# Pair weights loaded product by product, signs made on ScalarE, and a pause for weight sums: three edits to a fused attention and two feed-forward blocks

## The chip, the cores and the metric

The program runs on one core of a Trainium2 chip. Five engines work side by side, each through its own list of instructions in order: PE (TensorE, matrix products, with its weight loads shown as PEld), DVE (VectorE), ACT (ScalarE), POOL (GpSimd) and SP (SyncE, which here only issues DMA transfers). They meet at semaphores. The metric is the device time of one execution in microseconds (us).

## What is computed

The chunked attention of the reference gives 3072 tokens of width 512, which pass a gated block with 1536 hidden columns and then a second block with 2048:

```python
def _moe_ref(x, w_gate, w_val, w_out, rms_g):
    xn = x / np.sqrt(np.mean(x * x, axis=-1, keepdims=True) + 1e-06) * rms_g
    g = xn @ w_gate
    silu = g * (1.0 / (1.0 + np.exp(-g)))
    return silu * (xn @ w_val) @ w_out

def _moe2_ref(x, w_in, w_out):            # beta = 1
    h = x @ w_in
    g = np.where(h >= 1, h, np.where(h <= -1, 0.0, (h + 1) ** 2 / 4.0))
    return g @ w_out
```

## The kernel before, in words

**Numbers.** Every matrix product is split: each operand is a high part and a low part (the remainder), and three 128x128 by 128x512 matmuls stand for one product block. The weights arrive as float64, two 32-bit words for each number. A conversion takes an ACT pass over the high word (`conv_c` and `c`, lines 132 and 289, a scaled copy into a tile `tu`), three DVE operations that put exponent, sign and the low word's bits together (`join`, lines 142, 145, 148), an ACT copy that makes the high part (`hi`, line 292) and a DVE subtraction that makes the low part (`lo`, line 295).

**Token tiles.** The tokens form six tiles of 512. In the *single stage* (0 to about 518 us) four of them go through the first block one at a time: 12 feature steps `f`, each of three slots, with the attention of later tokens woven in between. The last two tiles, and all six tiles of the second block, go in pairs by a scheme with seven products in place of eight (`seven`): for each step the weights of seven products are needed, some of them sums and differences of weight blocks. The *pair input stage* of the first block (518 to 655 us) has 12 such units of 7 products of 6 matmuls; the *pair output stage* of it follows (to 718.7 us); then three pairs go through the second block (to 1194.4 us).

**Weight sums.** The seven weights of each unit (`w1p_d`, `w2p_d`, `w1o_d`, `w2o_d`) are made ahead of time by small steps: `at(n, fn)` puts a function on step `n`, and `conv_step(pace)` runs `pace` steps on average. In the last three single tiles each slot runs 2.8 steps, in the pair input stage each product runs `PACE2` steps; `conv_step(len(bg))` behind that stage runs all that is left. A group of 28 steps handles four float64 tiles of the second block: load (`load_w2`, POOL's queue), conversion, and two `pair_sums` of six steps (steps 10 to 15), whose results go to DRAM through POOL's queue. While a `pair_sums` is open, its name stands in `live`.

**Loading.** `load_wp(n)` brings the seven weights of unit `n` (1792 KB) through SP's queue into one half of a two-part buffer, which lies where the single tiles' weights of the features 9 to 11 were. It is issued at the end of unit `n - 2`. `load_wo` brings the output weights. The engines' orders are the order in which the code is written (`manual_schedule`), so an instruction that waits holds all that stand behind it on its engine; SP's and POOL's queues do the same with transfers.

In a unit, bank B starts as a copy of bank A (line 908, on ACT), the product in C is copied out (line 909, on ACT), and products are added on top:

```python
        product(n, A, 0, 0, True)
        product(n, C, 3, 2, True)
        p5 = tmp2("p5")
        nc.scalar.activation(B, A, AF.Copy)
        nc.scalar.activation(p5, C, AF.Copy)
        ...
        tt(out=C, in0=p5, in1=B, op=ALU.add)
```

Of the kernel before, what the change touches and what calls it, by code (L numbers as in the profile page):

```python
# [8 lines left out]
F32 = mybir.dt.float32  # L9
# [7 lines left out]
P = 128  # L17
# [16 lines left out]
D = 64  # L34
FILL = 352
PACE = 2.8
PACE2 = 0.9


@with_exitstack  # L40
def tile_stream_attention_moe_moe2(
# [85 lines left out]
    def conv_c():  # L127


        dst, key, w64 = raw.pop(0)  # L130
        tu = tmp.tile([P, 512], U32, tag="tu", name="tu")
        nc.scalar.activation(tu.bitcast(F32), words(w64)[1].bitcast(F32), AF.Copy, scale=2.0 ** -112)
        absd.append((dst, key, w64, tu))

    def words(w64):
        w = w64.rearrange("p (n two) -> p n two", two=2)
        return w[:, :, 0], w[:, :, 1]

    def join(tu, w64):

        lo64, hi64 = words(w64)
        nc.vector.tensor_scalar(
            out=tu, in0=tu, scalar1=3, scalar2=0x7FFFFFF8, op0=ALU.logical_shift_left, op1=ALU.bitwise_and
        )
        nc.vector.scalar_tensor_tensor(
            out=tu, in0=hi64, scalar=0x80000000, in1=tu, op0=ALU.bitwise_and, op1=ALU.bitwise_or
        )
        nc.vector.scalar_tensor_tensor(
            out=tu, in0=lo64, scalar=29, in1=tu, op0=ALU.logical_shift_right, op1=ALU.bitwise_or
        )  # L150
# [27 lines left out]


    G2 = F2 // 2  # L180
    w2p_d = [dram.tile([P, 2, 7, 256], F32, name=f"w2p_d{g}") for g in range(G2)]
    w2o_d = [dram.tile([P, 7, 2, 2, 256], F32, name=f"w2o_d{g}") for g in range(G2 // 2)]

    w1p_d = [dram.tile([P, 2, 7, 256], F32, name=f"w1p_d{f}") for f in range(F1)]
    w1o_d = [dram.tile([P, 7, 2, 2, 256], F32, name=f"w1o_d{k}") for k in range(F1 // 4)]


# [19 lines left out]
            nc.gpsimd.dma_start(dst(n, k), src.rearrange("p (k c) -> p k c", k=2))  # L209

    def in_dst(dp):
        return lambda n, k: dp[:, n, 3 + 2 * k:5 + 2 * k]

    def out_dst(do, u):
        return lambda n, k: do[:, (1, 4)[k]:(3, 6)[k], u, n]
# [42 lines left out]
    def w1_steps(i, f):  # L258
        g, v = (unit(3 * f + k).bitcast(F32) for k in range(2))
        dp = w1p_d[f]  # L260
        raws = [(dp[:, :, 0:2].rearrange("p h k c -> p h (k c)"), g), (dp[:, :, 2], v[:, :, 256:512])]
        sum_steps(i, (g, v), raws, rows_order, in_dst(dp))

    def w1o_steps(i, k):
# [15 lines left out]
    def w2_steps(g):  # L280

        dp, do, u = w2p_d[g], w2o_d[g // 2], g % 2
        f32_ = {}

        part = lambda j, n: w2raw[j][:, 512 * n:512 * n + 512]

        def c(j):
            f32_[j] = tmp.tile([P, 512], U32, tag="tu", name="tu")
            nc.scalar.activation(f32_[j].bitcast(F32), words(w2raw[j])[1].bitcast(F32), AF.Copy, scale=2.0 ** -112)

        def hi(j, n0, n1):
            nc.scalar.activation(part(j, 0)[:, n0:n1].bitcast(F32R), f32_[j].bitcast(F32)[:, n0:n1], AF.Copy)

        def lo(j, n0, n1, dsts):
            tt_(
                out=part(j, 1)[:, n0:n1].bitcast(F32),
                in0=f32_[j].bitcast(F32)[:, n0:n1],
                in1=part(j, 0)[:, n0:n1].bitcast(F32),
                op=ALU.subtract,
            )  # L300
            src = w2raw[j].bitcast(F32).rearrange("p (h c) -> p h c", h=2)
            for dst, c0, c1 in dsts:
                nc.gpsimd.dma_start(dst, src[:, :, c0:c1])

        dsts = [
            [(dp[:, :, 0:2].rearrange("p h k c -> p h (k c)"), 0, 512)],
            [(dp[:, :, 2], 256, 512)],
            [(do[:, 0, u], 0, 256)],
            [(do[:, 3, u], 0, 256), (do[:, 6, u], 256, 512)],
        ]  # L310
        for k in range(4):
            j, n = 4 * g + k, W2 + 28 * g + 7 * k
            n0, n1 = ((0, 512), (256, 512), (0, 256), (0, 512))[k]
            at(n, lambda j=j: c(j))
            at(n + 2, lambda j=j: join(f32_[j], w2raw[j]))
            at(n + 3, lambda j=j, n0=n0, n1=n1: hi(j, n0, n1))
            at(n + 5, lambda j=j, n0=n0, n1=n1, k=k: lo(j, n0, n1, dsts[k]))
            at(n + 10, lambda j=j: load_w2(j + 3))
        def pair_sums(a, b, n, order, dst):
            S, h = [], lambda: (f32_[a], f32_[b])  # L320

            def first():
                if m2["single"]:
                    S.extend([sp.tile([P, TT], F32, tag="s", name="s12"), sums_.tile([P, TT], F32, tag="s34", name="s34")])
                else:
                    S.extend(m2["late"][:, i] for i in range(2))
                S[:] = [x.rearrange("p (k c) -> p k c", k=2) for x in S]
                live.append(a)
                sums(S, *order(h()), True)

            at(n + 10, first)
            at(n + 11, lambda: sums(S, *order(h()), False))
            at(n + 12, lambda: hi_s(S, 0, f32_[a]))
            at(n + 13, lambda: hi_s(S, 1, f32_[b]))
            at(n + 14, lambda: lo_s(S, 0, f32_[a], dst))
            at(n + 15, lambda: (lo_s(S, 1, f32_[b], dst), live.remove(a)))

        pair_sums(4 * g, 4 * g + 1, W2 + 28 * g, rows_order, in_dst(dp))
        pair_sums(4 * g + 2, 4 * g + 3, W2 + 28 * g + 14, cols_order, out_dst(do, u))
# [442 lines left out]


    xb = wall[:, 0:14]
    wp = wall[:, 14:21].rearrange("p a b c -> p (a b c)").rearrange(
        "p (n h k c) -> p n h k c", n=2, h=2, k=7
    )
    wo = {}
    NP2 = NTT // 2

# [2 lines left out]
            nc.sync.dma_start(m2["y"][:, o], src[o])  # L793


    def load_wp(n):
        if n < F1 + NP2 * G2:
            src = w1p_d[n] if n < F1 else w2p_d[(n - F1) % G2]
            nc.sync.dma_start(wp[:, n % 2].bitcast(F32), src)

    def load_wo(i):

# [44 lines left out]
    for t in range(NS):  # L847
# [3 lines left out]
        for f in range(F1):  # L851
            if 0 < t < NS - 1 and f == 9:
                load_x(t + 1)
            if t == NS - 1 and f == F1 - 1:
                load_wp(0)
            proj_in(ps_g[0], w1[("g", f)])
            s = sp.tile([P, TT], F32, tag="s", name="s")
            nc.scalar.activation(s, ps_g[0], AF.Silu)  # L858
# [15 lines left out]
                out1(*pend)  # L874
            pend = (t, f)
            slot(t, 3 * f + 2)
    load_wp(1)

    b1, b2 = ps_g

    def product(n, bank, a, x, start):

        for kk in range(2):
            sl = slice(kk * P, kk * P + P)
            wh, wl = (wp[:, n % 2, i, a, sl] for i in range(2))
            xh, xl = (xb[:, 2 * x + kk, i] for i in range(2))
            st = start and kk == 0
            nc.tensor.matmul(bank, wh, xh, start=st, stop=False, skip_group_check=True)  # L888
            nc.tensor.matmul(bank, wh, xl, start=False, stop=False, skip_group_check=True)  # L889
            nc.tensor.matmul(bank, wl, xh, start=False, stop=kk == 1, skip_group_check=True)  # L890
        if n < F1:
            conv_step(PACE2)

    def tmp2(name):
# [5 lines left out]
    def seven(n, early):  # L900

        A, B, C, D, E = banks
        banks[:] = D, A, E, C, B
        tt = nc.vector.tensor_tensor
        product(n, A, 0, 0, True)
        product(n, C, 3, 2, True)
        p5 = tmp2("p5")
        nc.scalar.activation(B, A, AF.Copy)  # L908
        nc.scalar.activation(p5, C, AF.Copy)
        while defer:  # L910
            defer.pop(0)()
        product(n, B, 4, 1, False)
        product(n, A, 1, 4, False)
        tt(out=C, in0=p5, in1=B, op=ALU.add)
        done11 = early(A)
        product(n, B, 5, 3, False)
        tt(out=p5, in0=p5, in1=B, op=ALU.add)
        product(n, C, 6, 5, False)
        product(n, B, 2, 6, False)
        return done11, C, B, p5  # L920

    def t3(k):
# [3 lines left out]
    def proj1(f):  # L926
        k, u = divmod(f, 2)

        def silu(z):
            s = tmp2("s")  # L930
            nc.scalar.activation(s, z, AF.Silu)
            return s

        gate0, z12, z21, val1 = seven(f, silu)
        gate1 = silu(z12)
        tt_(out=m2["h"][:, k, u, 0], in0=gate0, in1=z21, op=ALU.mult)
        tt_(out=m2["h"][:, k, u, 1], in0=val1, in1=gate1, op=ALU.mult)
        if u:
            t3(k)
        load_wp(f + 2)  # L940

    def proj2(n):
        k = n % G2
# [157 lines left out]
    out1(*pend)  # L1101
    while live:
        conv_step(1)
    m2["single"] = False
    single_only.close()
    pair1 = moe1_only.enter_context(ExitStack())
    m2["pool"] = pair1.enter_context(tc.tile_pool(name="p1", bufs=1, reuse_waits="tile"))
# [144 lines left out]
```

## Time and profile before

| what | value |
|---|---|
| median of 3 runs | 1203.23 us (1202.67 to 1204.07) |
| the profiled execution's own time | 1202.52 us |
| its span in the trace | 1200.8 us |
| PE busy | 1144.0 us (95%) |
| DVE busy | 865.3 us (72%) |
| ACT busy | 620.2 us (52%) |
| POOL busy | 156.5 us (13%) |
| DMA moved | 281.76 MB, mean 235 GB/s |

A busy share is a mean over stages that have different limits, and a PE at half its clock is busy as well. So the table says which engine has the most to do, and not where time is lost; for that the span is cut into the stages named above.

### The profile page before, as it was taken

What the parts mean: (1) busy time and instruction counts of PE and PEld (TensorE: products, weight loads), DVE (VectorE), ACT (ScalarE), POOL (GpSimd) and SP (SyncE); (2) the same over time, 40 slices, a digit from 0 to 9 for tenths busy, and PEclk for the clock granted to TensorE, in tenths of its full rate; (3) what the DMA queues carried; (4) which work ended last, traced back from release to release, by engine and by line L of the source; (5) the groups of instructions that cost most, each with busy time, mean ns of one, the idle gap of its engine ahead of it and who ended that gap; (6) DMA issues with size and microseconds to landing.
All of it is one profiled execution on the core that took longest, in us unless ns stands there. A gap on an engine that the chain in (4) does not pass through costs nothing. (4 is left out here: it accounts for less than half of the span.)

```text
span 1200.8 us, 20562 instructions
## 1 busy us (share of the span) xinstructions
PE 1144.0 (95%) x7909; PEld 915.6 (76%) x7909; DVE 865.3 (72%) x1494; ACT 620.2 (52%) x1096; POOL 156.5 (13%) x239
## 2 busy tenths in 40 slices
PE   7889999999999999988998989999999999999998
PEld 4677878887777778766776868778887787887886
DVE  5888876676657767865655776787857888578855
ACT  4766756565666665433332644446534455444543
POOL 2200012231323233321221000000000000000000
PEclk8899999999999999998998999999999999999999
DMA  8565468898868777698896666656756476653465
GB/s 300 178 212 203 148 245 284 274 324 288 299 219 281 251 253 248 242 340 292 329 328 228 217 217 227 259 218 188 218 178 265 182 224 199 192 208 137 140 193 158
DMA packets 93968, 281.76 MB, mean 235 GB/s; under 512 B 11440, under 2 KB 34480, under 8 KB 87472
## 3 DMA queue, kind: packets, MB, share of 16 engines
q1 hardware_dynamic: 66992, 207.05, 51.2%
q0 software_dynamic: 19200, 65.03, 15.2%
q10 hardware_dynamic: 7680, 8.39, 2.0%
q8 instruction: 62, 1.02, 0.4%
q14 instruction: 34, 0.28, 0.1%
HBM read 201.26 MB, written 79.17 MB: 234 GB/s over the span
## 5 line engine op out<-in xcount | busy, mean ns | idle before, releaser
L1047 PE MATMUL ps_y<-r,wo 128*128 128x512 f32 x720 | 169.3, 391 | 2.6 <-DVE r L997 1.6
L997 DVE TENSOR_TENSOR r<-h,r 128x512 fp32r<-128x512 f32 x180 | 120.8, 688 | 54.4 <-ACT r L995 54.4
L1047 PEld LDWEIGHTS ps_y<-r,wo 128*128 128x128 f32 x720 | 134.3, 188 | 33.3 <-DVE r L997 3.3
L584 PE MATMUL ps_g<-xh,wall 128*128 128x512 f32 x384 | 157.1, 409 | 2.2 <-ACT s L858 2.1
L585 PE MATMUL ps_g<-xl,wall 128*128 128x512 f32 x384 | 151.1, 394 | 0.0
L586 PE MATMUL ps_g<-xh,wall 128*128 128x512 f32 x384 | 150.9, 393 | 0.0
L995 ACT ACTIVATE r<-h 128x512 fp32r<-128x512 f32 x180 | 108.3, 624 | 62.8 <-DVE h L986 15.0
L948 ACT ACTIVATE t<-t,half 128x512 f32<-128x512 f32 x96 | 66.9, 720 | 128.6 <-DVE t L947 128.6
L1047 PE MATMUL ps_g<-r,wo 128*128 128x512 f32 x540 | 127.4, 392 | 1.2 <-DVE r L997 1.1
L1047 PEld LDWEIGHTS ps_g<-r,wo 128*128 128x128 f32 x540 | 100.6, 188 | 24.9 <-DVE r L997 3.8
L888 PE MATMUL ps_g<-wall 128*128 128x512 f32 x198 | 80.4, 406 | 8.5 <-ACT ps_g L908 6.8
L584 PEld LDWEIGHTS ps_g<-xh,wall 128*128 128x128 f32 x384 | 73.0, 190 | 19.2 <-ACT s L858 2.9
L586 PEld LDWEIGHTS ps_g<-xh,wall 128*128 128x128 f32 x384 | 72.9, 190 | 16.5 <-DVE wall L117 0.4
L888 PE MATMUL ps_b<-wall 128*128 128x512 f32 x202 | 79.8, 395 | 5.2 <-DMA wall<-w1p_d 4.9
L585 PEld LDWEIGHTS ps_g<-xl,wall 128*128 128x128 f32 x384 | 73.0, 190 | 13.4
L584 PE MATMUL ps_y<-hh,wall 128*128 128x512 f32 x192 | 78.2, 407 | 2.8 <-ACT hh L116 2.8
L889 PE MATMUL ps_b<-wall 128*128 128x512 f32 x202 | 79.2, 392 | 0.0
L890 PE MATMUL ps_b<-wall 128*128 128x512 f32 x202 | 79.1, 392 | 0.0
L889 PE MATMUL ps_g<-wall 128*128 128x512 f32 x198 | 78.4, 396 | 0.0
L890 PE MATMUL ps_g<-wall 128*128 128x512 f32 x198 | 78.3, 395 | 0.0
L585 PE MATMUL ps_y<-hl,wall 128*128 128x512 f32 x192 | 75.7, 394 | 0.2 <-DVE hl L117 0.2
L586 PE MATMUL ps_y<-hh,wall 128*128 128x512 f32 x192 | 75.6, 394 | 0.0
(179 smaller groups left out, 2145.5 us busy)
## 6 DMA issues: line engine op xcount, KB each, us to landing
wo<-w2o_d SPq DMA_DIRECT2D x88, 512.0 KB, 3.7
wall<-w2p_d SPq DMA_DIRECT2D x24, 1792.0 KB, 7.3
wall<-w1p_d SPq DMA_DIRECT2D x12, 1792.0 KB, 10.2
w<-in_w_dram SPq DMA_DIRECT2D x36, 512.0 KB, 3.7
w<-in_w_dram POOLq DMA_DIRECT2D x32, 512.0 KB, 5.0
k_in<-in_k_dram SPq DMA_DIRECT2D x48, 256.0 KB, 4.7
wo<-w1o_d SPq DMA_DIRECT2D x21, 512.0 KB, 3.8
v_in<-in_v_dram SPq DMA_DIRECT2D x40, 260.0 KB, 4.4
```

Source lines behind the costliest of these rows:

```text
L584: nc.tensor.matmul(ps, wh, xh, start=start, stop=False)
L585: nc.tensor.matmul(ps, wh, xl, start=False, stop=False)
L586: nc.tensor.matmul(ps, wl, xh, start=False, stop=stop)
L888: nc.tensor.matmul(bank, wh, xh, start=st, stop=False, skip_group_check=True)
L889: nc.tensor.matmul(bank, wh, xl, start=False, stop=False, skip_group_check=True)
L890: nc.tensor.matmul(bank, wl, xh, start=False, stop=kk == 1, skip_group_check=True)
L948: nc.scalar.activation(s, s, AF.Square, scale=0.5, bias=half)
L995: nc.scalar.activation(r[:, 0], src, AF.Copy)
L997: tt_(out=r[:, 1], in0=src, in1=r[:, 0].bitcast(F32), op=ALU.subtract)
L1047: nc.tensor.matmul(bank[p][m], a, b, start=s0, stop=s1, skip_group_check=True)
```

## The change

Three things change together.

1. The pair weights lie in DRAM product by product (`[P, 7, 2, 256]` in place of `[P, 2, 7, 256]`), and are loaded one product (256 KB) at a time into a ring of 14. The load of product `i + 14` stands right behind product `i`. Eight loads are issued at the last feature step of the last single tile and six behind it. The writes of the sums into DRAM follow the new layout in runs of 1 KB where they had 2 KB, and the two writes of raw weights into such a unit become three.
2. The ACT pass over the high word uses `Prelu`, whose slope for negative input is 2^32. This moves the exponent of a negative number so that the shift by 3 puts a bit into the sign's place; `join` loses its sign operation, and has two DVE operations in place of three.
3. In the last seven slots of the last single tile no step is run unless a `pair_sums` is open. `PACE2` goes from 0.9 to 0.95, and each `load_w2` stands three steps later in its group.

```diff
-PACE2 = 0.9
+PACE2 = 0.95
...
-        nc.scalar.activation(tu.bitcast(F32), words(w64)[1].bitcast(F32), AF.Copy, scale=2.0 ** -112)
+        nc.scalar.activation(tu.bitcast(F32), words(w64)[1].bitcast(F32), AF.Prelu, scale=2.0 ** -112, alpha=2.0 ** 32)
...
-        nc.vector.tensor_scalar(
-            out=tu, in0=tu, scalar1=3, scalar2=0x7FFFFFF8, op0=ALU.logical_shift_left, op1=ALU.bitwise_and
-        )
-        nc.vector.scalar_tensor_tensor(
-            out=tu, in0=hi64, scalar=0x80000000, in1=tu, op0=ALU.bitwise_and, op1=ALU.bitwise_or
-        )
+        nc.vector.tensor_scalar(out=tu, in0=tu, scalar1=3, scalar2=None, op0=ALU.logical_shift_left)
...
-    w1p_d = [dram.tile([P, 2, 7, 256], F32, name=f"w1p_d{f}") for f in range(F1)]
+    w1p_d = [dram.tile([P, 7, 2, 256], F32, name=f"w1p_d{f}") for f in range(F1)]
...
-            at(n + 10, lambda j=j: load_w2(j + 3))
+            at(n + 13, lambda j=j: load_w2(j + 3))
...
             m2["pace"] -= 1
+            if m2["hold"] and not live:
+                continue
...
+            m2["hold"] = t == NS - 1 and s >= 29
             conv_step(PACE)
...
-    def load_wp(n):
+    def load_wp(i):
+        n, j = divmod(i, 7)
         if n < F1 + NP2 * G2:
             src = w1p_d[n] if n < F1 else w2p_d[(n - F1) % G2]
-            nc.sync.dma_start(wp[:, n % 2].bitcast(F32), src)
+            nc.sync.dma_start(wp[:, i % 14].bitcast(F32), src[:, A_OF[j]])
...
             if t == NS - 1 and f == F1 - 1:
-                load_wp(0)
+                for i in range(8):
+                    load_wp(i)
...
-        if n < F1:
+        load_wp(i + 14)
+        if i < 7 * F1:
             conv_step(PACE2)
```

Where the steps go follows from the paces. Before, 304 steps stand ahead of the pair input stage, the other 72 lie in it, and none is left behind it. After, 282 stand ahead of it, 80 lie in it, and the last 17 run in one piece behind it.

On DVE, at the end of the pair input stage, before (`h` are the hidden values, `y` the next tile's input, `r` the ring from which the output products read):

```order
L936 TENSOR_TENSOR h<-t_6062,ps_g_108 128x512
L937 TENSOR_TENSOR h<-t_6061,t_6057 128x512
L924 TENSOR_TENSOR h<-h 128x512
L834 TENSOR_TENSOR y<-y 128x1024
L997 TENSOR_TENSOR r_6067<-h,r_6067 128x512
L999 TENSOR_TENSOR h<-h 128x512
```

The same place on DVE after the change:

```order
L926 TENSOR_TENSOR h<-h 128x512
L290 TENSOR_TENSOR w_6762<-tu,w_6762 128x256
L142 TENSOR_SCALAR tu<-tu 128x512
L143 SCALAR_TENSOR_TENSOR tu<-w_6833,tu 128x512
L192 TENSOR_TENSOR s_5971<-tu 128x256
L193 TENSOR_TENSOR s_5971<-tu 128x256
L195 TENSOR_TENSOR s_5971<-s_5971,tu 128x256
L196 TENSOR_TENSOR s_5971<-tu,s_5971 128x256
L290 TENSOR_TENSOR w_6833<-tu,w_6833 128x512
L202 TENSOR_TENSOR s_5971<-s_5971,tu 128x512 x2
L833 TENSOR_TENSOR y<-y 128x1024
L997 TENSOR_TENSOR r_5982<-h,r_5982 128x512
```

Ten operations of the left-over steps now stand between the last hidden values and the first ring entry of the output stage.

On SP, at the passage from the single tiles to the pair, before (`ys` is the last single tile's result, `wo` the output weights):

```order
L799 DMA wall_102<-w1p_d0_132 128x3584
L799 DMA wall_102<-w1p_d1_133 128x3584
L618 DMA y_d3_113<-ys_6034 128x2048
L815 DMA wo_6075<-w1o_d0_144 128x1024
L815 DMA wo_6077<-w1o_d1_145 128x1024
L815 DMA wo_6079<-w1o_d2_146 128x1024
L815 DMA wo_6081<-w1o_d0_144 128x1024
L799 DMA wall_102<-w1p_d2_134 128x3584
```

The same place on SP after the change:

```order
L798 DMA wall_102<-w1p_d0_132 128x512 x7
L798 DMA wall_102<-w1p_d1_133 128x512 x7
L613 DMA y_d3_113<-ys_5957 128x2048
L814 DMA wo_5990<-w1o_d0_144 128x1024
L814 DMA wo_5992<-w1o_d1_145 128x1024
L814 DMA wo_5994<-w1o_d2_146 128x1024
L814 DMA wo_5996<-w1o_d0_144 128x1024
L798 DMA wall_102<-w1p_d2_134 128x512 x7
```

The places are the same; each load of a unit has become seven, each of which stands behind one product of two units earlier.

On ACT, in the last two feature steps of the single stage, before (`s` is the gate, `hh` the high part of the hidden values, `w` a float64 tile of the second block):

```order
L292 ACTIVATE w_5766<-tu 128x512
L858 ACTIVATE s<-ps_g_108 128x512
L204 ACTIVATE tu<-s_5884 128x512
L204 ACTIVATE tu<-s_5885 128x512
L116 ACTIVATE hh<-s 128x512
L824 ACTIVATE wall<-y 128x2x512
L289 ACTIVATE tu<-w_5838 128x512
L292 ACTIVATE w_5838<-tu 128x512
L858 ACTIVATE s<-ps_g_108 128x512
```

The same place on ACT after the change:

```order
L823 ACTIVATE wall<-y 128x2x512
L858 ACTIVATE s<-ps_g_108 128x512
L116 ACTIVATE hh<-s 128x512
L823 ACTIVATE wall<-y 128x2x512
L858 ACTIVATE s<-ps_g_108 128x512
L116 ACTIVATE hh<-s 128x512
```

The conversions and sums between the gates and the hidden values are gone from there.

## Rows read from the trace of the kernel before

**Rows 1.** Busy time by stage: stretch, length, each engine, granted clock, DMA share, GB/s.

```profile
498.00:518.00 20.00, 15.09 (x51) 11.29 (x50) 17.83 (x30) 8.05 (x14) 6.16 (x9) 0.84 0.89 323
518.00:655.00 137.00, 121.61 (x506) 97.20 (x505) 76.63 (x133) 47.78 (x86) 30.68 (x47) 0.95 0.84 302
655.00:718.70 63.70, 60.35 (x254) 46.63 (x253) 49.25 (x70) 33.30 (x53) 0.00 (x0) 1.00 0.69 218
718.70:1194.40 475.70, 473.00 (x2106) 385.70 (x2104) 355.11 (x552) 226.18 (x364) 0.00 (x0) 1.00 0.60 201
```

**Rows 2.** Timeline of PE in the single stage's last steps: start, length, work, idle before.

```profile
500.23 0.50 PE L584 MATMUL ps_g<-xh,wall 128*128 128x512 f32 x1 [1.90 <-ACT s L858]
```

**Rows 3.** Timeline of ACT just ahead of it.

```profile
499.06 0.63 ACT L292 ACTIVATE w<-tu 128x512 fp32r<-128x512 f32 x1 [2.73 <-issue]
499.60 0.58 ACT L858 ACTIVATE s<-ps_g 128x512 f32<-128x512 f32 x1
```

**Rows 4.** Busy time of PE alone behind that wait: busy, clock, DMA share, GB/s.

```profile
501.00:504.50 3.50, 3.50 (x10) 0.54 0.99 415
```

**Rows 5.** Waits of PE in the pair input stage: total us, times, longest.

```profile
PE ps_g L888 <- ACT ps_g L908: 6.8, 2, 5.0
PE ps_b L888 <- DMA wall<-w1p_d: 4.9, 1, 4.9
```

**Rows 6.** Timeline of SP's queue in that stage.

```profile
531.66 1.34 SPq L815 DMA_DIRECT2D wo<-w1o_d  x3
533.11 7.33 SPq L799 DMA_DIRECT2D wall<-w1p_d  x2
```

**Rows 7.** Timeline of ACT, POOL and DVE in that stage.

```profile
524.35 0.60 ACT L909 ACTIVATE t<-ps_b 128x512 f32<-128x512 f32 x1 [1.52 <-DMA y_d<-ys]
...
618.95 0.56 POOL L276 DMA_DIRECT2D w<-in_w_dram  x1 [10.77 <-DMA w2p_d<-w]
...
628.97 0.66 ACT L289 ACTIVATE tu<-w 128x512 f32<-128x512 f32 x1 [4.16 <-DMA w2p_d<-tu]
...
634.72 0.43 DVE L197 TENSOR_TENSOR s<-tu 128x256 f32<-128x256 f32 x1
634.77 0.63 ACT L292 ACTIVATE w<-tu 128x512 fp32r<-128x512 f32 x1 [4.13 <-issue]
```

**Rows 8.** Groups by line and shape, whole span: busy us, mean ns, idle before.

```profile
L145 DVE SCALAR_TENSOR_TENSOR tu<-w,tu 128x512 uint32<-128x512 uint32 x68 | 48.6, 717 | 1.6
L142 DVE TENSOR_SCALAR tu<-tu 128x512 uint32<-128x512 uint32 x68 | 28.9, 429 | 14.6 <-ACT tu L289 9.5 <-ACT tu L132 5.0
L289 ACT ACTIVATE tu<-w 128x512 f32<-128x512 f32 x32 | 21.2, 662 | 15.7 <-DMA w2p_d<-tu 7.4 <-DMA w2o_d<-tu 5.1 <-DMA w<-in_w_dram 3.2
L948 ACT ACTIVATE t<-t,half 128x512 f32<-128x512 f32 x96 | 66.9, 720 | 128.6 <-DVE t L947 128.6
```

**Rows 9.** Transfers of the pair input stage: all, then one kind, us to landing.

```profile
DMA packets 7211, 41.35 MB, mean 302 GB/s; under 512 B 1073, under 2 KB 1073, under 8 KB 5397
...
w2p_d<-tu POOLq DMA_DIRECT2D x6, 256.0 KB, 7.9
```

**Rows 10.** Transfers issued in the first 20 us, us to landing.

```profile
k_in<-in_k_dram SPq DMA_DIRECT2D x8, 256.0 KB, 4.9
```

**Rows 11.** Busy time by stretch in the opening, columns as in rows 1.

```profile
10.00:15.00 5.00, 2.53 (x107) 1.83 (x110) 2.05 (x4) 1.78 (x3) 0.00 (x0) 0.82 1.06 396
```

**Rows 12.** Timeline of DVE at the start of the pair output stage.

```profile
657.05 1.22 DVE L834 TENSOR_TENSOR y<-y 128x1024 f32<-128x1024 f32 x1
658.19 0.68 DVE L997 TENSOR_TENSOR r<-h,r 128x512 fp32r<-128x512 f32 x1
```

**Rows 13.** Waits of PE from 40 to 489 us, first and last of eight rows.

```profile
PE ps_a L557 <- ACT xn L573: 3.3, 1, 3.3
...
PE ps_a L461 <- ACT x_nat L573: 0.6, 1, 0.6
```

**Rows 14.** Timeline of ACT ahead of one of these waits.

```profile
416.30 0.42 ACT L292 ACTIVATE w<-tu 128x256 fp32r<-128x256 f32 x1 [2.59 <-DVE tu L148]
```

More of the change, by code (lines that the diff above doesn't have):

```diff
@@ L139, in join @@
     def join(tu, w64):
-        lo64, hi64 = words(w64)
-        nc.vector.tensor_scalar(
-            out=tu, in0=tu, scalar1=3, scalar2=0x7FFFFFF8, op0=ALU.logical_shift_left, op1=ALU.bitwise_and
-        )
-        nc.vector.scalar_tensor_tensor(
-            out=tu, in0=hi64, scalar=0x80000000, in1=tu, op0=ALU.bitwise_and, op1=ALU.bitwise_or
-        )
+        lo64 = words(w64)[0]
+        nc.vector.tensor_scalar(out=tu, in0=tu, scalar1=3, scalar2=None, op0=ALU.logical_shift_left)
         nc.vector.scalar_tensor_tensor(
@@ L180, in tile_stream_attention_moe_moe2 @@
     G2 = F2 // 2
-    w2p_d = [dram.tile([P, 2, 7, 256], F32, name=f"w2p_d{g}") for g in range(G2)]
+    w2p_d = [dram.tile([P, 7, 2, 256], F32, name=f"w2p_d{g}") for g in range(G2)]
     w2o_d = [dram.tile([P, 7, 2, 2, 256], F32, name=f"w2o_d{g}") for g in range(G2 // 2)]
-    w1p_d = [dram.tile([P, 2, 7, 256], F32, name=f"w1p_d{f}") for f in range(F1)]
+    w1p_d = [dram.tile([P, 7, 2, 256], F32, name=f"w1p_d{f}") for f in range(F1)]
     w1o_d = [dram.tile([P, 7, 2, 2, 256], F32, name=f"w1o_d{k}") for k in range(F1 // 4)]
@@ L211, in in_dst @@
     def in_dst(dp):
-        return lambda n, k: dp[:, n, 3 + 2 * k:5 + 2 * k]
+        return lambda n, k: dp[:, 3 + 2 * k:5 + 2 * k, n]
     def out_dst(do, u):
@@ L260, in w1_steps @@
         dp = w1p_d[f]
-        raws = [(dp[:, :, 0:2].rearrange("p h k c -> p h (k c)"), g), (dp[:, :, 2], v[:, :, 256:512])]
+        raws = [(dp[:, k], w[:, :, c:c + 256]) for k, w, c in ((0, g, 0), (1, g, 256), (2, v, 256))]
         sum_steps(i, (g, v), raws, rows_order, in_dst(dp))
@@ L288, in c @@
             f32_[j] = tmp.tile([P, 512], U32, tag="tu", name="tu")
-            nc.scalar.activation(f32_[j].bitcast(F32), words(w2raw[j])[1].bitcast(F32), AF.Copy, scale=2.0 ** -112)
+            nc.scalar.activation(f32_[j].bitcast(F32), words(w2raw[j])[1].bitcast(F32), AF.Prelu, scale=2.0 ** -112, alpha=2.0 ** 32)
         def hi(j, n0, n1):
@@ L305, in w2_steps @@
         dsts = [
-            [(dp[:, :, 0:2].rearrange("p h k c -> p h (k c)"), 0, 512)],
-            [(dp[:, :, 2], 256, 512)],
+            [(dp[:, 0], 0, 256), (dp[:, 1], 256, 512)],
+            [(dp[:, 2], 256, 512)],
             [(do[:, 0, u], 0, 256)],
@@ L339, in w2_steps @@
         pair_sums(4 * g + 2, 4 * g + 3, W2 + 28 * g + 14, cols_order, out_dst(do, u))
-    m2 = {"single": True, "pace": 0.0}
+    m2 = {"single": True, "pace": 0.0, "hold": False}
     for j in range(F1 // 2):
@@ L784, in tile_stream_attention_moe_moe2 @@
     xb = wall[:, 0:14]
-    wp = wall[:, 14:21].rearrange("p a b c -> p (a b c)").rearrange(
-        "p (n h k c) -> p n h k c", n=2, h=2, k=7
-    )
+    wp = wall[:, 14:21].rearrange("p a b c -> p (a b c)").rearrange("p (s h c) -> p s h c", s=14, h=2)
+    A_OF = (0, 3, 4, 1, 5, 6, 2)
+    X_OF = (0, 2, 1, 4, 3, 5, 6)
     wo = {}
@@ L876, in tile_stream_attention_moe_moe2, with product @@
             slot(t, 3 * f + 2)
-    load_wp(1)
+    for i in range(8, 14):
+        load_wp(i)
     b1, b2 = ps_g
-    def product(n, bank, a, x, start):
+    def product(i, bank, start):
+        x = X_OF[i % 7]
         for kk in range(2):
-            sl = slice(kk * P, kk * P + P)
-            wh, wl = (wp[:, n % 2, i, a, sl] for i in range(2))
-            xh, xl = (xb[:, 2 * x + kk, i] for i in range(2))
+            wh, wl = (wp[:, i % 14, h, kk * P:kk * P + P] for h in range(2))
+            xh, xl = (xb[:, 2 * x + kk, h] for h in range(2))
             st = start and kk == 0
@@ L904, in seven @@
         tt = nc.vector.tensor_tensor
-        product(n, A, 0, 0, True)
-        product(n, C, 3, 2, True)
+        product(7 * n, A, True)
+        product(7 * n + 1, C, True)
         p5 = tmp2("p5")
@@ L911, in seven @@
             defer.pop(0)()
-        product(n, B, 4, 1, False)
-        product(n, A, 1, 4, False)
+        product(7 * n + 2, B, False)
+        product(7 * n + 3, A, False)
         tt(out=C, in0=p5, in1=B, op=ALU.add)
         done11 = early(A)
-        product(n, B, 5, 3, False)
+        product(7 * n + 4, B, False)
         tt(out=p5, in0=p5, in1=B, op=ALU.add)
-        product(n, C, 6, 5, False)
-        product(n, B, 2, 6, False)
+        product(7 * n + 5, C, False)
+        product(7 * n + 6, B, False)
         return done11, C, B, p5
@@ L1103, in tile_stream_attention_moe_moe2 @@
         conv_step(1)
-    m2["single"] = False
+    m2["single"] = m2["hold"] = False
     single_only.close()
```

2 lines of the change are left out of this document (removed).

## The prediction

> **What bounds the kernel now.** I read the table of stages first. Behind 718.7 us PE issues 2106 matmuls in 475.7 us, 0.226 us each, with the clock at full rate [rows 1]: that is the pace at which nothing but PE counts, and the measure for the stages ahead of it. The last 20 us of the single stage hold 51 matmuls, 11.5 us at that pace, so 8.5 us are lost. The pair input stage has 12 x 7 x 6 = 504 matmuls, 113.9 us, and takes 137.0: 23.1 lost. The pair output stage has 252, 57.0 us, and takes 63.7: 6.7 lost [rows 1]. The three pairs of the second block lose nothing. So the time to be won lies between 498 and 719 us, and next to it in the waits of the long single stage.
>
> What ends last in each place is read from waits and timelines. In the single stage's end PE waits for ACT's gate [rows 2]; ACT had stood 2.73 us in a copy of the background conversion, and took the gate right behind it [rows 3]. After such a wait the granted clock averages 0.54 over 3.5 us (mostly the lower level, 1.2 GHz), while PE is busy throughout [rows 4], so a wait of 2 us costs over 3 us. In the pair input stage PE's waits sum to 15.3 us in six rows, of which I show the first two [rows 5]; the half clock and short delays make up the rest of 23.1. The 4.9 us wait is for a weight load: SP came to it at 533 us, behind output-weight loads that left only at 531.66, and 1792 KB then had to land whole [rows 6]. The 5.0 us wait names ACT's copy, but ACT was held by the background: its conversion waited 4.16 us for a store of an older `tu`, and the next copy 4.13 us more [rows 7]. That store was late because POOL's queue had stood 10.77 us in a load that waited for another store [rows 7]. The transfers are no simple bound: share 0.84 and 302 GB/s in the mean [rows 1].
>
> **The change, part by part.**
>
> *Sign by slope.* `join` loses one DVE operation of 0.717 us, 68 times: 48.6 us of DVE [rows 8]. Most of it lies beside PE's work and is worth nothing. What counts is where a join stands ahead of what PE waits for, as in [rows 14], where ACT waits 2.59 us for it. From 40 to 489 us PE waits 13.5 us in all (eight rows, ten waits, of which I show the first and the last) [rows 13]. If every wait shrank by one operation, 7.2 us would go; if the joins are beside the chain, none. About half of these chains pass a join, so I take 4. The slope itself is one ACT pass of the same shape; the trace has no such function. Its nearest rows are the scaled copy, 0.662 us, and a pass with a bias tile, 0.720 [rows 8]: 0 to 4 us of ACT in 68 passes, on an engine that is busy 35% of the pair input stage [rows 1]; I take 0. The order shows no table load more than before.
>
> *The pause.* From slot 29 on about 22 steps are gone from DVE, ACT and POOL, and with them the copies that stood ahead of the last gates and hidden values. What is left on DVE there is the gate product, the low part and a few operations on the next tile. I take 8.0 of the 8.5 us, with 5 as the low end, because the next tile's operations remain. The work is not saved: 8 steps more run in the pair input stage, and 17 behind it.
>
> *The 17 steps behind the stage.* On DVE they are ten operations ahead of the first ring entry: five of half width at about 0.4 us, a shift of 0.43, four of full width at about 0.7 [rows 7, 8, 12], some 5.0 us in sequence. Before, the entry for block 4 is ready at 658.19 + 0.68 = 658.9 [rows 12]. PE has four blocks ahead, 24 matmuls or 5.4 us from 655.0, so it needs that entry at 660.4: 1.5 us in hand. After it comes 5.0 late, a wait of 3.5 us. The next entries pass at a DVE pace close to PE's, so about 1 us more is lost, and a half clock of 3 us costs 1.5. That is +5.8. If the queue behind it catches up it is 0; if the last tile's load is late as well, 8. This term is a loss.
>
> *The ring.* A load is now issued right behind the product that frees its place, and has 13 products, 17.6 us, to land; before, a whole unit's load had one unit, 9.5 us, if SP came to it at once. SP's blocked output-weight loads should leave early, as no sums are open when the pair stage begins. An issue costs SP 0.45 us (three in 1.34) [rows 6] against a product of 1.36, so SP keeps up. The waits for loads go. The later `load_w2` gives the store it waits for some 7 steps, 10 us, so POOL's queue should no longer stand; this removes the cause of the 5.0 us wait. What stays: the first unit waits for the store of the last single tile before `p5` can be written [rows 7], 1.8 us, and transfers still run near their limit. The stage moved 41.35 MB [rows 9]; a group of 28 steps reads 2.1 MB and writes 3.7, so eight steps add 1.6, and some of the first loads shift in. 43 to 44 MB at between 323 GB/s, as at the single stage's end [rows 1], and 396 [rows 11] take 110 to 135 us, less what the full ring lends. So PE and transfers are nearly level, and I add 5 us of short waits: 113.9 + 1.8 + 5.3 = 121, a gain of 16. Ends: 116 and 132.
>
> Here a rule speaks against the change. In the opening, transfers of 256 KB take 4.9 us each to land [rows 10], and yet 396 GB/s flow [rows 11]: several are in flight. The Trainium skill, page "DMA: Bandwidth & Descriptors", section "Rules for kernel authors", asks for at least 1 MiB in each transfer, and its section on the anatomy of a DMA gives a fixed 2.0 us plus bytes over 436 GB/s (for the GpSimd path). By that, one at a time, my estimate is 2.6 us a product and 218 us for the stage. The opening's rows disagree as long as transfers overlap. By them I stay with 121.
>
> *Nothing else.* In the second block's pairs the loads take the same new form at a share of 0.60 [rows 1]; I take 0 there.
>
> Sum: -4.0 - 8.0 - 16.0 + 5.8 = -22.2. The profiled execution took 1202.5 us, so 1180.3; the median of the runs is 0.7 above it, which gives 1181. I say **1180**.
>
> **Rivals.**
>
> *The transfers become the bound.* If the small runs bring the pair input stage's rate down to the 323 GB/s of [rows 1], its 43 MB take 133 us, the gain there is 4, and the time is 1193. For it: share 0.84 already, stores of 256 KB that take 7.9 us to land [rows 9]. Against: 415 GB/s in a stretch of mixed traffic [rows 4]. Chance 0.13.
>
> *All of it goes.* The pair stage runs at 116 us, the single stage's waits shrink by 6, and the 17 steps cost 3: 1181 - 5 - 2 - 3 = 1171 or a little below. Chance 0.10.
>
> *Small loads come too late.* SP's transfers use eight counters in turn, so a load waits for the eighth one before it. If each takes L us to land, products follow at L / 8. Above 10.9 us PE waits for every one of 84 products, and at 13.9 the stage takes 146 us, from where the kernel is slower; at 16 us it is 168, and the time 1181 + 47 = 1228. For it: 7.9 us for stores of this size under load [rows 9]; against it: 4.9 at full share [rows 10]. The rule above would push this way. Chance 0.04.
>
> *The waits only move.* DVE and ACT stay as jerky as before, since 80 steps now lie in the pair input stage where 72 did, and each late conversion still holds ACT. Then that stage gains only the load waits, some 8 us with their half clock, the tail 5, the middle nothing, and the steps behind cost 5.8: -7. New waits for `tu` of that size bring it to 0: 1196 to 1203. Chance 0.05.
>
> **How the numbers follow.** My forecast has 0.68 and by itself reaches from 1172 to 1190. To leave out 0.2, the range takes in the second rival and most of the first: 1167 to 1194. A measurement here tells 0.2%, 2.4 us, from no change. Faster: 0.68 + 0.13 + 0.10 and half of the last, 0.93; same 0.03; slower 0.04.
>
> **What would show it.** Right: the copies ahead of the last gates gone from 490 us on and the granted clock at 1.0 there; the pair input stage at 116 to 126 us with no wait for `w1p_d` over 1 us; POOL's waits for `w2p_d` stores near nothing; a wait of PE for the ring some 5 us into the output stage, which takes 68 to 71 us. The slope pass shows 0.66 to 0.72 us. Wrong: long waits for loads of 256 KB, or ACT held again by conversions in the pair input stage.

## The result and the profile after

The changed kernel takes 1183.97 us (median of 4 runs, 1180.98 to 1186.25) against 1202.95 us (4 runs, 1195.26 to 1204.07): ratio 0.985, 95% interval 0.981 to 0.990. One run of the kernel before, 1195.26, lies 7 us below its three others, and the interval is wide for it. The forecast was 1180, range 1167 to 1194. The profiled execution of after took 1184.7 us, 17.8 less than that of before.

The stages of after, with the columns of [rows 1]; each of the last three starts with its first matmul:

```profile
40.00:484.00 444.00, 434.24 (x4291) 347.44 (x4290) 303.15 (x599) 279.32 (x525) 116.72 (x164) 0.99 0.75 249
484.00:504.20 20.20, 20.20 (x90) 16.70 (x89) 14.15 (x17) 9.73 (x15) 3.79 (x6) 1.00 0.74 256
504.20:629.80 125.60, 118.48 (x505) 95.87 (x504) 73.98 (x131) 48.24 (x88) 35.18 (x51) 0.97 0.97 344
629.80:701.30 71.50, 63.42 (x253) 48.30 (x252) 54.22 (x80) 36.52 (x59) 5.83 (x8) 0.95 0.69 218
701.30:1177.00 475.70, 473.05 (x2105) 385.81 (x2103) 355.19 (x552) 226.53 (x365) 0.00 (x0) 1.00 0.67 202
```

Against [rows 1]: the single stage ends at 504.2 in place of 518.0, and PE is busy in all of its last 20.2 us at full clock. The pair input stage takes 125.6 us in place of 137.0, the pair output stage 71.5 in place of 63.7, the second block's pairs 475.7 as before. That is -13.8 -11.4 +7.8 = -17.4.

PE's waits in the pair input stage, the two largest of five (before: [rows 5]):

```profile
PE ps_g L889 <- DVE ps_b L916: 4.3, 1, 4.3
PE ps_g L889 <- DVE t L919: 1.4, 1, 1.4
```

No wait for a load is left. The largest is in the first unit. Its timeline on SP, PE, ACT and DVE (start, length, work; in brackets the idle time before and what ended it):

```profile
505.19 0.32 SPq L613 DMA_DIRECT2D y_d<-ys  x1
...
509.44 0.39 PE L891 MATMUL ps_g<-wall 128*128 128x512 f32 x1
...
511.88 0.60 ACT L911 ACTIVATE t<-ps_b 128x512 f32<-128x512 f32 x1 [5.51 <-DMA y_d<-ys]
...
511.90 0.43 DVE L192 TENSOR_TENSOR s<-tu 128x256 f32<-128x256 f32 x1 [5.71 <-DMA y_d<-ys]
...
513.37 0.69 DVE L916 TENSOR_TENSOR ps_b<-t,ps_g 128x512 f32<-128x512 f32 x1
...
514.11 0.79 PE L889 MATMUL ps_g<-wall 128*128 128x512 f32 x1 [4.28 <-DVE ps_b L916]
```

ACT's copy into `p5` (L911) and DVE's first background sum (L192, into `s1234`) both go into memory that the last single tile's `ys` held, and wait for its store. PE needs L916, which stands on DVE behind four of these sums. Behind the wait the clock is at the lower of its two levels (1.2 in place of 2.4 GHz), and again, for nearly all of the stretch, behind the wait at the start of the output stage (busy time of PE alone; the last three numbers are granted clock, DMA share and GB/s):

```profile
514.00:519.50 5.50, 5.39 (x13) 0.50 1.03 400
...
638.80:643.00 4.20, 2.90 (x6) 0.52 0.75 258
```

The transfers of the pair input stage (before: [rows 9]), all and the ring's loads:

```profile
DMA packets 17790, 43.25 MB, mean 344 GB/s; under 512 B 2248, under 2 KB 2248, under 8 KB 17399
...
wall<-w1p_d SPq DMA_DIRECT2D x70, 256.0 KB, 6.1
```

At the start of the output stage, DVE and PE (before: [rows 12]). Four blocks of PE run from 629.83; then it waits for the ring entry of L995 and L997, which stand behind the left-over steps (L192 to L290 here, others left out):

```profile
633.55 0.42 DVE L192 TENSOR_TENSOR s<-tu 128x256 f32<-128x256 f32 x1
635.79 0.42 DVE L193 TENSOR_TENSOR s<-tu 128x256 f32<-128x256 f32 x1 [1.82 <-DMA w2p_d<-s]
...
638.92 1.22 DVE L833 TENSOR_TENSOR y<-y 128x1024 f32<-128x1024 f32 x1
640.05 0.69 DVE L997 TENSOR_TENSOR r<-h,r 128x512 fp32r<-128x512 f32 x1
...
629.83 5.60 PE L1047 MATMUL ps_y<-r,wo 128*128 128x512 f32 x24
638.85 0.70 PE L1047 MATMUL ps_y<-r,wo 128*128 128x512 f32 x1 [3.42 <-ACT r L995]
```

The groups of the conversion (before: [rows 8]). The slope pass takes 663 and 670 ns, as the scaled copy did:

```profile
L132 ACT ACTIVATE tu<-w 128x512 f32<-128x512 f32 x36 | 23.9, 670 | 13.5 <-DMA w<-in_w_dram 12.6 <-DVE tu L143 0.8
...
L284 ACT ACTIVATE tu<-w 128x512 f32<-128x512 f32 x32 | 21.2, 663 | 4.1 <-DMA w2o_d<-tu 3.7 <-DMA w2p_d<-tu 0.4
```

### The profile page after: what moved, and what is told of

Read it like the earlier page. It is cut to its first block, busy times and chain, and to the rows that moved or that the text cites. A ratio compares the mean times of both kernels' runs of the same rounds, so it can differ in the third digit from the quotient of the medians.

```text
span 1182.9 us, 21015 instructions
## 1 busy us (share of the span) xinstructions
PE 1137.3 (96%) x7909; PEld 913.3 (77%) x7909; DVE 822.6 (70%) x1426; ACT 621.6 (53%) x1096; POOL 175.1 (15%) x247
## 4 chain that ended last, share of the span: by engine, by line
PE 75%; DVE 10%; ACT 6%; DMA 4%; issue 3%; SPq 1%; POOL 0%; ACTq 0%; DVEq 0%; POOLq 0%
PE ps_y L1047 12%; PE ps_g L1047 9%; PE ps_g L579 6%; PE ps_g L580 6%; PE ps_g L581 6%; PE ps_y L579 3%; PE ps_g L889 3%; PE ps_b L889 3%; PE ps_y L580 3%; PE ps_y L581 3%; PE ps_b L891 3%; PE ps_b L890 3%; PE ps_g L891 3%; PE ps_g L890 3%; PE ps_y L889 2%
## 5 line engine op out<-in xcount | busy, mean ns | idle before, releaser
L1047 PE MATMUL ps_y<-r,wo 128*128 128x512 f32 x720 | 172.5, 396 | 7.3 <-ACT r L995 4.4
L997 DVE TENSOR_TENSOR r<-h,r 128x512 fp32r<-128x512 f32 x180 | 120.8, 687 | 54.5 <-ACT r L995 54.5
L995 ACT ACTIVATE r<-h 128x512 fp32r<-128x512 f32 x180 | 108.4, 626 | 60.8 <-DVE r L997 14.5
L889 PE MATMUL ps_g<-wall 128*128 128x512 f32 x198 | 79.1, 400 | 7.8 <-DVE ps_b L916 4.3
L891 PE MATMUL ps_g<-wall 128*128 128x512 f32 x198 | 77.7, 392 | 0.0
L890 PE MATMUL ps_g<-wall 128*128 128x512 f32 x198 | 77.6, 392 | 0.0
```

The lines of the kernel that those rows point to most:

```text
L995: nc.scalar.activation(r[:, 0], src, AF.Copy)
L997: tt_(out=r[:, 1], in0=src, in1=r[:, 0].bitcast(F32), op=ALU.subtract)
L1047: nc.tensor.matmul(bank[p][m], a, b, start=s0, stop=s1, skip_group_check=True)
```

## The experiments

My theory was the prediction's sum: slope, pause, ring and left-over steps each act in a place of their own. The rivals: transfers set the input stage, and the waits only move. All kernels start from the changed one. In the table the third tile is the time between SP's issues of the second and the third single tile's store, the stages are read from PE's first matmuls to about 0.2 us, and ratios are to the kernel before on the same chip.

| kernel | third tile | single stage ends | input stage | output stage | time | ratio (95%) |
|---|---|---|---|---|---|---|
| before | 123.8 | 517.9 | 137.0 | 63.7 | 1203.0 | 1 |
| after | 120.6 | 504.2 | 125.6 | 71.5 | 1184.0 | 0.985 (0.981 to 0.990) |
| without the slope | 122.6 | 507.6 | 125.5 | 70.5 | 1188.2 | 0.989 (0.987 to 0.991) |
| without the pause | 120.6 | 514.6 | 132.6 | 63.7 | 1191.5 | 0.991 (0.989 to 0.994) |
| whole units | 120.7 | 505.0 | 134.0 | 75.1 | 1196.4 | 0.995 (0.993 to 0.997) |
| 1.2 steps a product | 120.6 | 505.1 | 140.2 | 63.7 | 1190.9 | 0.990 (0.987 to 0.993) |
| ring laid out first | 120.6 | 504.0 | 118.7 | 71.3 | 1177.2 | 0.979 (0.977 to 0.982) |
| ring of 7 | 120.6 | 506.5 | 130.1 | 70.9 | 1193.1 | 0.990 (0.988 to 0.993) |
| 0.7 steps a product | 120.6 | 504.4 | 124.1 | 94.2 | 1208.1 | 1.004 (1.002 to 1.005) |
| early `load_w2` | 122.1 | 509.1 | 123.6 | 73.0 | 1187.6 | 0.987 (0.985 to 0.989) |
| ring first, steps spread | 120.7 | 504.3 | 118.3 | 66.2 | 1172.3 | 0.975 (0.972 to 0.977) |
| 1.2 steps, small loads | 120.6 | 502.2 | 133.9 | 63.7 | 1183.9 | 0.985 (0.983 to 0.988) |

Tiles and stages come from one profiled execution of each kernel, while whole executions of one kernel spread by 2 to 10 us (the widest, the ring of 7: 1185.6 to 1195.9, and its profile is of the slowest). The third tile repeats within 0.2 us wherever its code is the same, the input stage within 0.5 (the two kernels with the ring laid out first). The first tile does not (its store leaves between 160.2 and 165.4 us), so differences there say nothing. Not undone by any run: the layout in DRAM, and the pace of 0.95 where before had 0.9.

**Without the slope.**

```diff
-        nc.scalar.activation(tu.bitcast(F32), words(w64)[1].bitcast(F32), AF.Prelu, scale=2.0 ** -112, alpha=2.0 ** 32)
+        nc.scalar.activation(tu.bitcast(F32), words(w64)[1].bitcast(F32), AF.Copy, scale=2.0 ** -112)
...
+        nc.vector.scalar_tensor_tensor(
+            out=tu, in0=hi64, scalar=0x80000000, in1=tu, op0=ALU.bitwise_and, op1=ALU.bitwise_or
+        )
```

> The changed kernel with the scaled copy and the join of three operations back (68 more DVE operations of 0.717 us), all else as changed. My theory (a join stands ahead of what PE waits for in about half of the waits of the long single stage): the matmul that stands at 489 us comes 4 us later, the 17 steps behind the pair input stage cost 1 us more, time 1184 + 5 = 1189. Rival, the joins lie beside the chain and the lead of 4.3 us at 489 us came from elsewhere (the later load of the second block's weights, say): nothing moves, 1184.

The time is 4.2 us up, though the two intervals overlap. What repeats is the third tile, 1.9 us longer; SP's stores at its two ends without the slope:

```profile
285.82 0.33 SPq L618 DMA_DIRECT2D y_d<-ys  x1
...
408.37 0.33 SPq L618 DMA_DIRECT2D y_d<-ys  x1
```

and in after:

```profile
284.17 0.33 SPq L613 DMA_DIRECT2D y_d<-ys  x1
...
404.80 0.33 SPq L613 DMA_DIRECT2D y_d<-ys  x1
```

The rest of the 3.4 us at the single stage's end arose in the first tile and can't be put down to the slope. The output stage did not get longer, against my 1 us.

**Early `load_w2`.**

```diff
-            at(n + 13, lambda j=j: load_w2(j + 3))
+            at(n + 10, lambda j=j: load_w2(j + 3))
```

> The changed kernel with the load of the second block's weights again 10 steps behind their conversion in place of 13. My theory: POOL's queue stands again some 10 us in such a load while the stores behind it wait, conversions that need their buffers hold ACT, and one wait of 3 to 5 us returns in the pair input stage: 128 to 131 us, time 1187 to 1190. Rival, with the loads of the ring small and early the stores land soon enough anyway: 125 us, 1184 (or less, as the loads come earlier).

POOL's queue stands again in the input stage, 24.5 us in four waits for stores, of which after has none there:

```profile
POOL w L271 <- DMA w2p_d<-w: 12.5, 2, 7.3
POOL w L271 <- DMA w2o_d<-w: 12.0, 2, 6.6
```

But no wait of PE came back with it: the stage is 2 us shorter than in after. The kernel is 3.6 us slower. Of that 1.5 us are the third tile's, which repeats; the last tile's 0.5 lies within what the same code differs there (99.4 to 100.1 us in six runs), and the rest of what the profile shows is mostly the first tile's. So the later load does help, by about 1.5 us and in another place than I had put it, and the 5.0 us wait of [rows 5] did not hang on POOL's queue alone.

**Without the pause.**

```diff
-            m2["hold"] = t == NS - 1 and s >= 29
+            m2["hold"] = False
```

> The changed kernel without the pause, so 304 steps stand ahead of the pair input stage, 75 in it and none behind it. My theory: the last 15 us of the single stage lose their 9 us again (copies of the background stand ahead of the last gates), and the pair output stage gets back its 7.8 us because no step is left for it; together 1185, so pause and left-over steps as good as cancel. Rival A, the tail was helped by the shorter join and not by the pause: tail stays, 1176. Rival B, the pair output stage is longer for another cause than the left-over steps: it stays at 71 us, 1193.

From the third tile's store to the stage's end it takes 108.7 us, in after 99.4, in before 108.2: the pause is worth 9.3 us there, and without left-over steps the output stage is at 63.7. Both as I held. What I had not foreseen is the input stage, 7 us longer with five steps fewer in it. DVE at the stage's start:

```profile
515.98 0.43 DVE L193 TENSOR_TENSOR s<-tu 128x256 f32<-128x256 f32 x1 [3.83 <-DMA w2o_d<-s]
...
517.46 1.28 DVE L600 COPY ys<-ps_y 128x512 f32<-128x512 f32 x2
```

A background sum waits for a store, and the last tile's eviction stands behind it. Its store is issued 4.8 us after the stage has begun (in after 1.0), and PE waits 4.7 us in the first unit; another wait for the same copy, 2.6 us, ends at 629 us. So the pause also clears the entry of the input stage, a gain that my sum did not have.

**Whole units.** The ring becomes two halves, each loaded in one transfer, which the end of `proj1` issues:

```diff
+            s = 7 * (n % 2)
+            nc.sync.dma_start(wp[:, s:s + 7].bitcast(F32), src)
...
-        load_wp(i + 14)
...
+        load_wp(f + 2)
```

> The changed kernel with whole units loaded again (seven products, 1792 KB, in one transfer into one of two halves, issued behind the unit), the new layout in DRAM and all else kept. My theory: PE waits for these loads again, 4.9 us and some short ones with their half clock, and the pair input stage goes from 125.6 to about 134 us: 1192. Rival, the stage is set by the sum of its transfers (share 0.97, 344 GB/s) and not by when each one lands: the same bytes, the same 125 us, 1184.

The stage is 8.4 us longer, as expected, but not by the waits that I named: those for `w1p_d` are only 1.1 us. The largest new ones, 4.3 us in the input stage and 7.7 in the output stage (there by way of ACT), lead back to DVE, which stood in a background sum:

```profile
584.62 0.43 DVE L193 TENSOR_TENSOR s<-tu 128x256 f32<-128x256 f32 x1 [4.43 <-DMA w2o_d<-s]
584.97 0.68 DVE L916 TENSOR_TENSOR t<-t,ps_g 128x512 f32<-128x512 f32 x1
...
649.13 0.42 DVE L193 TENSOR_TENSOR s<-tu 128x256 f32<-128x256 f32 x1 [6.14 <-DMA w2p_d<-s]
```

The stores of 256 KB that DVE waits for left at 574.71 us, beside a load of 1792 KB and two of 1024 KB, and at 639.97, behind a load of 1792 KB; they landed 9.9 and 9.1 us later. In after the same two stores took 7.4 and 5.1 us. DVE, which needs their buffers, holds what PE needs. The run changes the size of a load and the moment of its issue together, so which of the two makes the stores late is not shown. The rate is lower, 320 GB/s in place of 344, but the bytes are the same and the stage is longer: the DMA share is 0.88 in place of 0.97, and divided by it the rates are 364 and 355. The Trainium skill, page "DMA: Bandwidth & Descriptors", section "Rules for kernel authors", asks for 1 MiB and more in a transfer; with several transfers in flight, no clear loss from 256 KB shows here.

**Ring of 7.**

```diff
-            nc.sync.dma_start(wp[:, i % 14].bitcast(F32), src[:, A_OF[j]])
+            nc.sync.dma_start(wp[:, i % 7].bitcast(F32), src[:, A_OF[j]])
...
+        load_wp(i + 7)
```

> The changed kernel with a ring of 7 products in place of 14, so a load has 6 products or 8.1 us to land in place of 13. My theory: what mattered is that a load is one product and is issued when its place comes free; the loads land in 6.1 us in the median, a few come late, input stage 127 us, 1184 to 1187. Rival, the length of the ring carried the gain (loads are held up for long by the stores between them): waits for w1p_d return with their half clock, input stage 133 us or more, 1192.

The rival held, more or less: 130.1 us, with two waits for loads (4.1 and 1.8 us), and the second block's first input stage, 78.6 us in after, takes 83.7. Behind two 1024 KB loads of `y` on SP (568.69 us) the loads of w1p_d issued from 560 to 586 us land late; us from issue to landing:

```profile
DMA to landing us min/median/max: 7.8/9.3/14.5
```

A ring of 7 gives them 8.1 us, one of 14 gives 17.6. The median over the stage, 5.2 us, would not have told it.

**More and fewer steps in the input stage.** Only the number of background steps for each product changes, 0.95 to 1.2 (97 steps in the stage, none left) and to 0.7 (59 in it, 38 left).

> The changed kernel with 1.2 steps for each product in place of 0.95, so all 97 steps that stand behind the single stage lie in the pair input stage and none behind it. My theory (PE and its waits set that stage, and the left-over steps cost the output stage 7.8 us): input stage 126 to 128 us, output stage 64 us, time 1176 to 1178. Rival, transfers set the input stage at 344 GB/s: 17 more steps bring 17/28 of 5.8 MB, 3.5 MB or 10 us, the stage takes 136 us, time 1186.

> The changed kernel with 0.7 steps for each product, so 59 steps lie in the pair input stage and 38 behind it. Theory A, from the run with 1.2 steps for each product (17 more steps, 14.6 us more in the stage, 0.86 us a step): background steps set the short waits of the input stage; with 21 fewer it takes 115 to 118 us, and the output stage at 7.8/17 us a step 9.6 more, 81 us; time 1183 to 1187. Theory B, as I predicted, PE and the first unit set the input stage and the steps in it are covered: 125 us still, and the output stage 81: 1194.

With 1.2 the output stage is at 63.7, so the left-over steps are what cost 7.8 there; but the input stage grows by 14.6 us, more than theory (at most 2.4) or rival (10) gave. With 0.7 it is only 1.5 us shorter than with 0.95 (nearer to theory B than to A's 115 to 118), so up to there the steps are nearly covered. The 38 left-over steps cost 30.5 us, not the 17.4 (7.8 + 9.6) of both theories: in sequence they wait for their own transfers, and PE stands for 26.2 us. ACT in that time:

```profile
642.35 0.66 ACT L284 ACTIVATE tu<-w 128x512 f32<-128x512 f32 x1 [6.96 <-DMA w2o_d<-tu]
...
649.89 0.66 ACT L284 ACTIVATE tu<-w 128x512 f32<-128x512 f32 x1 [2.27 <-DMA w<-in_w_dram]
...
654.33 0.66 ACT L284 ACTIVATE tu<-w 128x512 f32<-128x512 f32 x1 [1.97 <-DMA w2p_d<-tu]
```

**Why 1.2 costs 14.6.** One of its waits, on ACT, DVE and PE:

```profile
574.04 0.67 ACT L284 ACTIVATE tu<-w 128x512 f32<-128x512 f32 x1 [2.11 <-DMA w<-in_w_dram]
...
579.92 0.42 ACT L287 ACTIVATE w<-tu 128x256 fp32r<-128x256 f32 x1 [4.20 <-issue]
580.24 0.58 ACT L910 ACTIVATE ps_g<-ps_b 128x512 f32<-128x512 f32 x1
...
578.69 0.42 DVE L142 TENSOR_SCALAR tu<-tu 128x512 uint32<-128x512 uint32 x1
...
580.87 0.50 PE L889 MATMUL ps_g<-wall 128*128 128x512 f32 x1 [2.76 <-ACT ps_g L910]
```

The join behind the conversion's first pass (L142) meets DVE's five operations at a unit's end and starts at 578.69, ACT's next copy (L287) waits for it, and the copy that PE needs (L910) stands behind that. The first pass is late as well, by a load. To tell the order from a want of bandwidth, the ring's loads were cut:

```diff
-            nc.sync.dma_start(wp[:, i % 14].bitcast(F32), src[:, A_OF[j]])
+            e = 32 if 14 <= i < 7 * F1 else 256
+            nc.sync.dma_start(wp[:, i % 14, :, 0:e].bitcast(F32), src[:, A_OF[j], :, 0:e])
```

> The run with 1.2 steps for each product (input stage 140 us), with the 70 later loads of its ring cut to an eighth of their columns, so that 16 of its 46 MB go; the rest of each ring place keeps old weights, which leaves the product wrong. Theory A, the order of the conversions on ACT and DVE sets its short waits (a gap of PE for ACT's copy, which stands behind a conversion, which stands behind DVE's join, which stands behind the unit's own operations): the stage stays at 134 to 140 us, time 1185 to 1191. Theory B, transfers set it: it falls to 126 us or less, time 1177 or less.

The stage moves 30.2 MB in place of 46.3 and takes 133.9 us, 6.3 less, where theory A's range began. The same wait stands in the same place with the same length, though the first pass is now early and waits for nothing:

```profile
569.63 0.66 ACT L284 ACTIVATE tu<-w 128x512 f32<-128x512 f32 x1
...
575.95 0.42 DVE L142 TENSOR_SCALAR tu<-tu 128x512 uint32<-128x512 uint32 x1
...
578.14 0.50 PE L890 MATMUL ps_g<-wall 128*128 128x512 f32 x1 [2.76 <-ACT ps_g L911]
```

So the order alone makes this wait, and the load's 2.11 us has no part in it. In all, 8.3 of the 14.6 us stay with a third of the bytes gone and the order on ACT and DVE as it was, and 6.3 hang on the transfers: PE's waits are 2.4 us fewer and its busy time, at a higher clock, 3.9. A wait that did hang on a load is this one of the run with 1.2 steps, where a first pass stands right ahead of L910; in the run with small loads that pass waits 0.35 us and PE not at all:

```profile
614.26 0.66 ACT L284 ACTIVATE tu<-w 128x512 f32<-128x512 f32 x1 [2.08 <-DMA w<-in_w_dram]
...
615.46 0.50 PE L889 MATMUL ps_y<-wall 128*128 128x512 f32 x1 [1.30 <-ACT ps_y L910]
```

The order also speaks on the 5.0 us wait of the kernel before. There the copy L292 that held ACT until 634.77 [rows 7] had its join behind the same five operations, of which the last and the join's first are

```profile
632.21 0.69 DVE L999 TENSOR_TENSOR h<-h 128x512 f32<-128x512 f32 x1
632.82 0.42 DVE L142 TENSOR_SCALAR tu<-tu 128x512 uint32<-128x512 uint32 x1
```

Four of before's L908 have such a copy right ahead of them on ACT; of after's L910, the same copy of bank A, none has. Which step falls there follows from the pace and the order, so the new pace, or the pause, may be what took the wait away. Neither is shown: no run has 0.9 with all else as changed, and without the pause a wait of 2.6 us for this copy stands near the same place.

**Ring laid out first.**

```diff
+        m2["ring"] = [new([P, 2, TT], f"r{i}", F32R) for i in range(n_ring)]
         m2["t"], m2["n"] = [new([P, TT], f"t{i}") for i in range(n_t)], 0
-        m2["ring"] = [new([P, 2, TT], f"r{i}", F32R) for i in range(n_ring)]
...
+    second_pool(F1 // 2, 5, 6)
     m2["late"] = m2["pool"].tile([P, 2, TT], F32, name="s1234")
-    second_pool(F1 // 2, 5, 6)
```

> The changed kernel with the buffers of the pair stages laid out in another order: the ring of the output stage first, where the last single tile's ys lies, and the buffers t and s1234 behind it, so that the copy into p5 and the background's sums no longer wait for the store of ys. My theory: the 4.3 us wait of the first unit goes to under 0.5 us and with it some 2 us of half clock; the pair input stage takes 119 to 121 us, time 1178 to 1180. Rival, transfers set that stage (share 0.97): what the first unit wins is lost in waits behind it, 125 us, 1184.

The busy times of its input stage:

```profile
504.00:622.70 118.70, 115.73 (x506) 94.20 (x505) 74.10 (x131) 48.30 (x88) 35.23 (x51) 1.00 0.99 365
```

6.9 us fewer, the clock at 1.00, and as many bytes at 365 GB/s. The rival falls: 344 GB/s was not a limit of the transfers but what PE, held up, asked for, though the DMA share was 0.97 then and is 0.99 now.

**Ring first, steps spread.** In place of the 17 steps ahead of the output stage, half a step for each block:

```diff
                 self.split(n + L)
+                conv_step(0.5)
...
-    conv_step(len(bg))
```

> The ring laid out first, as in the run before, and the 17 left-over steps no longer issued in one piece ahead of the output stage: half a step for each of its 42 blocks. My theory: these steps cost 7.8 us because they stand in sequence ahead of the first ring entries on DVE and ACT; spread, they lie beside PE, which needs DVE for some 49 of 64 us there, and the output stage takes 64 to 67 us: time 1177 - 6 = 1170 to 1173. Rival, DVE has no room there, since each ring entry is needed at PE's pace: the steps cost their DVE time wherever they stand, 70 us, 1176.

```profile
622.60:688.80 66.20, 61.12 (x254) 46.52 (x253) 53.84 (x80) 35.76 (x59) 5.81 (x8) 1.00 0.73 235
```

The output stage takes 66.2 us (columns as above), 5.1 less than with the steps in one piece; 2.5 us of their price are left, in short waits for ring entries. At 1172.3 us this version beats both kernels, at 0.975 of the kernel before.

## Why the prediction was right, and where it was off

The direction and the places were right; the time came out 4 us above the forecast.

- **The slope, -4.0.** The middle of the single stage won 3.1 us, all in the third tile. Undoing the slope gives back 1.9 of it, undoing the later load 1.5. So the term holds two causes, of which I had named one; 1.8 us more came in the first tile, where runs of the same code differ by 5, which is luck. The pass itself costs nothing, as taken.
- **The pause, -8.0.** 8.7 us from the last tile; its PE has no wait left, where I had left 0.5 for the next tile's operations. That it also clears the entry of the input stage was in no term of mine.
- **The ring, -16.** The mis-sized term: the input stage gives -11.4, and that is not the ring's alone, as the stage is 7.0 us longer without the pause and 8.4 longer with whole units; the two overlap. The loads' waits are gone, and the short waits and delays are 4.6 us against my 5.3. What failed is "1.8 us" for the first unit, which I took from the wait before `p5` in [rows 7] (the row shows 1.52). It is 7.1: 4.4 from 509.44 to 514.11 less one matmul of 0.23, and 2.7 behind it, where 13 matmuls take 5.6 us in place of 2.95. In after the store that `p5` waits for runs beside six ring loads issued just ahead of it and lands after 6.6 us, and DVE's sums into `s1234` wait for it too, ahead of L916. In the ring of 7, where no loads go just ahead of it, it lands after 5.0 us and PE waits 2.7. Taking the shared memory away gave 6.9 us back. The reason that I gave for the end of the 5.0 us wait (the later load) fell with the early load's run: the wait came at least in part from the order on DVE and ACT, and what took it away is not isolated. Loading by products, small and early (whole units are 8.4 us worse), and a ring that is long enough (7 places are 4.5 worse) both carry the gain.
- **The left-over steps, +5.8.** Measured +7.8. The wait for the ring entry is 3.4 us (predicted 3.5), the next one 1.25, the clock 0.52 behind them. I had the sequence right but took it as DVE time alone; 1.82 us of it is a wait for a store. My three parts, 3.5, 1 and 1.5, sum to 6.0 and not to 5.8.
- **The rivals.** "The transfers become the bound" and "Small loads come too late" are refuted by 365 GB/s and landings of 6.1 us with 14 places. With 7 places loads do come too late, but because their places come free only 8.1 us ahead; the median landing (5.2 us, 9.3 in the worst stretch) stays under the 10.9 us that this rival asked for. "The waits only move" is close to what 1.2 steps a product does: the input stage is 3.2 us longer than before.

## What to carry to other kernels

When a stage begins, look up whose memory its first buffers take over: a store of 1 MB that lands some 6.6 us after its issue held two engines, and another order of the allocations freed them at no cost. Background work on engines that serve PE was nearly free here up to a density and then cost more than its own time (17 steps more: 5.0 us of DVE, 14.6 of the stage), in part because a step that waits behind a unit's last operations holds the copy that PE needs next. Left in one piece it runs at the pace of its own transfers; spread it over all stages that have room. Size a ring of loads by the slowest landing in the stage, not by the median.

## What was not expected of the hardware

With the ring laid out first, and its loads and the stores of 256 KB on two queues, the input stage moved 365 GB/s in the mean over 118.7 us, at a DMA share of 0.99. A share near 1 did not mean that the transfers set the time: at 0.97 the same bytes had flowed at 344 GB/s, and PE's waits were the cause. With the ring of 7 the landing of one such load ranged from 7.8 to 14.5 us in one stretch of the stage, where the median over all of it was 5.2.
